# Luna attention and SMeLU feed-forward: seven add-and-max passes of batches 0 and 1 on GpSimd, and a shared clock for GpSimd's loads and passes in the planner

## The chip, the cores and the metric

One Trainium2 chip, one core. The metric is the device time of one execution in microseconds (us), the median of the runs; less is better. The engines are named PE (TensorE, matrix products), DVE (VectorE), ACT (ScalarE), POOL (GpSimd) and SP (SyncE, which only issues transfers). Each works through its own queue in order, and they wait for each other on semaphores.

## The reference

```python
# q, k, v: (8, 8, 576, 64), p: (8, 8, 32, 64), all float32
def sm_attn(qq, kk, vv):                    # softmax attention, scale 1/8
    s = scale * np.matmul(qq, kk.transpose(0, 1, 3, 2))
    a = np.exp(s - np.max(s, axis=-1, keepdims=True))
    a = a / (np.sum(a, axis=-1, keepdims=True) + 1e-09)
    return np.matmul(a, vv)
p_packed = sm_attn(p, k, v)                 # 32 landmarks look at 576 keys
x = sm_attn(q, p_packed, p_packed)          # 576 queries look at the landmarks
x = x.transpose(0, 2, 1, 3).reshape(4608, 512)
h = x @ w_in                                # 512 -> 2048
g = np.where(h >= 1, h, np.where(h <= -1, 0.0, (h + 1) ** 2 / 4))   # SMeLU
out = g @ w_out                             # 2048 -> 512, (4608, 512) float32
```

## The kernel before, in words

There are eight batches of 576 tokens. For each batch the kernel turns k and q (`kT`, `qT`), makes the scores of the landmarks (`sp`, `ex`), the packed values (`pk`, `ppT`), the scores of the queries and their softmax (`s2`, `eT`, `sm`, `ln`, `rc`, `A`). Instead of the attention's output it then forms M = packed values times w_in (`mp`, evicted to `M`), so that the hidden layer is h = A times M directly.

The hidden layer of a batch is worked in KF = 16 tiles fi of 128 hidden units by 576 tokens, each in the function `hidden`, by four steps:

- `mm` (L649, PE): four matmuls into the PSUM tile h
- `low` (L655, ACT): x = Prelu(h - 1) with slope 0.5, from PSUM to float32 in SBUF
- `cut` (L663 on DVE or L665 on ACT): t = max(x + 1, 0), float32 from SBUF to SBUF. This is the add-and-max pass.
- `last` (L670, DVE): min(t, 1) * t, written as bfloat16 into hT

The result is the SMeLU: for h above 1 it is 1 * h, between it is t * t with t = (h + 1) / 2. In batch 0 the first two tiles (`SPLIT = 2`) are worked in two halves of 288 tokens each. An output tile (function `output`, L723) takes 128 tokens of hT and sums 16 matmuls, one for each fi, into the PSUM tile o. It is evicted to ob by ACT or DVE (L197, the line of the helper `copy`) and stored by SP (L741). Batches are paired; a pair has nine output tiles of 128 tokens.

The order of all work is written by a planner (`Task`, `Plan`) before anything is emitted. Each step is a task with a rank, the tasks that it needs, the buffers that it takes, and its possible engines, each with how long the engine is kept and when the result is there. `Plan.run` simulates the engines, and always gives the engine that is free first the lowest rank that is ready. The order found is the order in which the instructions are emitted, so every engine's queue is fixed by it, and so is the engine of each step with a choice (t among them: DVE or ACT). The ranks come from constants: `H1, H2` and `PITCH0, PITCH1` for the hidden tiles, `T1, T2` and the offsets beside them for the attention of batches 1 and 2, `L1` for the landmarks of batches 2 to 7, `M1` for the pitch of M's groups in batch 0, `EARLY` for the output tiles that belong to batches 0 and 1 (start and span of each one's 16 matmuls).

Nearly all loads are issued from GpSimd's queue (`G_.dma_start`, L274 for k, q and v, L285 and L290 for the weights, L293 for p). The plan keeps their clock under the name DMA (0.78 us for an issue) and GpSimd's one other task, `make_identity`, under POOL: two clocks for one engine. Where the plan expects PE to wait before the first output matmul, `warm` puts products of zeros (L791) into PE's queue; here they are called filler.

```python
t_t = plan.add(r + 0.02, {"DVE": (0.16 + 0.3 / n, 0.156 + 0.3 / n, part(cut)),
                          "ACT": (0.12 + 0.48 / n, 0.21 + 0.48 / n, part(cut))}, [t_x], ...)
```

Here n is 2 for a tile that is worked in halves and 1 otherwise.

Of the kernel before, what the change touches and what calls it, by code (L numbers as in the profile page):

```python
# [24 lines left out]
class Plan:  # L25
# [25 lines left out]
    def run(self, slack):  # L51
        waiting = {id(t): len(t.deps) + len(t.behind) for t in self.tasks}
        for t in self.tasks:
            for d in t.deps + t.behind:
                d.users.append(t)
        ready = [t for t in self.tasks if not waiting[id(t)]]
        done = []
        while ready:
            best = None
            found = defaultdict(list)  # L60
            left = {b: sorted(v) for b, v in self.slots.items()}
            for t in sorted(ready, key=lambda t: t.rank):
                at = max((d.end + self.LATENCY for d in t.deps), default=0.0)
                at = max([at] + [d.start + 0.001 for d in t.behind])
                need = defaultdict(int)
                for b in t.takes:
                    need[b] += 1
                short = any(len(left[b]) < n for b, n in need.items())
                wants = at < self.free["PE"] + self.CLAIM
                for b, n in need.items():  # L70
                    if not short:
                        at = max(at, left[b][n - 1] + self.LATENCY)
                    if wants:
                        del left[b][:n]
                if short:
                    continue
                for e in t.ways:
                    found[e].append((max(self.free[e], at), t))
            for e, some in found.items():
                first = min(x[0] for x in some)  # L80
                at, t = min((x for x in some if x[0] <= first + slack.get(e, 0.0)), key=lambda x: (x[1].rank, x[0]))
                if best is None or at < best[0]:
                    best = at, t, e
            assert best is not None, "no step can take its buffers"
            at, t, e = best
            if e == "PE" and t.mode != self.mode:
                at = max(at, self.free[e] + self.SWITCH)
            ready.remove(t)
            keep, lasts = t.ways[e][:2]
            t.start, t.engine = at, e  # L90
            if e == "DMA":
                begin = max(self.pipe, at + lasts)
                self.pipe = begin + t.ways[e][3]
                t.end = self.pipe + t.ways[e][4]
            else:
                t.end = at + lasts
                if len(t.ways[e]) > 3:

                    beside = self.pipe > at + 1.5
                    self.pipe = max(self.pipe, at + 1.5) + t.ways[e][3] * (1.4 if beside else 1.0)  # L100
                    t.end = max(t.end, self.pipe + t.ways[e][4] * (2.0 if beside else 1.0))
            self.free[e] = at + keep
            if e == "PE":
                self.mode = t.mode
            for b in t.takes:
                self.slots[b].remove(min(self.slots[b]))
            for box in t.frees:
                box[0] -= 1
                box[1] = max(box[1], t.end)
                if box[0] == 0:  # L110
                    self.slots[box[2]].append(box[1])
            done.append(t)
            for u in t.users:
                waiting[id(u)] -= 1
                if waiting[id(u)] == 0:
                    ready.append(u)
        assert len(done) == len(self.tasks)
        return sorted(done, key=lambda t: t.start)
# [3 lines left out]
def kernel(  # L122
# [14 lines left out]
    ALU = mybir.AluOpType  # L137
# [19 lines left out]
    MB1 = {("w_in", 0, 0): 0.7, ("w_in", 0, 1): 0.7}  # L157
    FIRST = 2
    PAIRED = 2
    SPLIT, AHALF, WPARTS, MPARTS, QLATE, ORDER3, ORDER, MERGE = 2, 0, 1, 2, 0, 4, 2, 2  # L160
    Q0 = [range(0, 8, 2), range(1, 5, 2), range(5, 9, 2)]
    LOADS = "k0 v0 q0 win0 win1 win2 k1 wout0 v1 wout1 win3 wout2 q1 wout3 q2 v2 k2 p"
    H1, H2 = 22.12, 44.98
    PITCH0, PITCH1 = 2.02, 0.20
    T1, T2 = -12.12, 26.79
    LENT = [2, 5]
    L1, M1 = -0.94, -0.23
    KT1, QT1 = -5.40, 11.05
    SC1, PK1 = 23.87, 1.56
    ST1, MT1 = 34.14, 40.50  # L170
    EARLY = [[(11.06, 92.69), (49.64, 36.28), (46.46, 38.0), (38.16, 25.3)], [(56.52, 5.8), (23.31, 23.03), (58.69, 13.54), (38.34, 20.24), (1.0, 50.02)]]

    V, A_, G_ = nc.vector, nc.scalar, nc.gpsimd
    nc.scalar.preload_act_table_set("natural_log_exp_and_others")
# [14 lines left out]
    plan = Plan(dict(BUFS, dma=8))  # L189
# [167 lines left out]
    def attention(b, at, fine):  # L357
# [110 lines left out]
        def packed(e):  # L468
# [15 lines left out]
            for g in range(G):  # L484
                for c in range(NC):
# [3 lines left out]
        t = plan.add(at["pk"], {"PE": (1.01, 1.18, packed) if paired else (1.28, 1.45, packed)},  # L489
                     [ready["ex0"], ready["ex1"], consts] + (pairs if paired else landed["v", b, 0]),  # L490
                     ["w", "ppT"], mode=None if paired else "pk")
# [43 lines left out]
        for gs in [[0], [1]] if fine else [[0, 1]]:  # L535
            needs = {id(t): t for g in gs for h in range(g, H, G) for t in ready["q", h]}

            def small(e, gs=gs):
                probs(gs)
                if merged:  # L540
# [3 lines left out]
            t = plan.add(at["s2"] + 0.01 * gs[0], {"PE": (long, long + 0.15, small)},  # L544
                         (pp if len(gs) > 1 else [pp[gs[0]]]) + list(needs.values()) + [landed["w_in", 3]] * merged,
                         ["w", "eT"] * len(gs) + ["w", "M"] * merged, mode="s")
# [6 lines left out]
        for g in range(G):  # L553
# [24 lines left out]
            r = at["sm"] + 0.2 * g  # L578
# [6 lines left out]
            n = 2 if AHALF and b == 0 else 1  # L585
# [32 lines left out]
        for fs in groups:  # L618

            parts = [[0], [1]] if WPARTS and (b, fs) == (0, [0]) else [[0, 1]]  # L620
            r = at["M"] + at.get("M+", 2.0) * fs[0]
            copies = defaultdict(list)
            for i, gs in enumerate(parts):
                needs = [landed["w_in", 0, g] if WPARTS and f == 0 else landed["w_in", f] for f in fs for g in gs]
                t = plan.add(r + 0.02 * i, {"PE": (0.24 * len(fs), 0.24 * len(fs) + 0.17,
                                                   lambda e, fs=fs, gs=gs: project(fs, gs))},
                             pp + needs, ["w"] * len(fs) * (i == 0) + (["M"] if (fs[0], i) == (0, 0) else []),
                             mode="s", behind=[before])
                before = t
                mms.append(t)  # L630
                for f in fs:
                    copies[f] += taken(r + 0.02 * i, t, f, gs)
            for f in fs:
                plan.release("w", copies[f])
# [6 lines left out]
    def hidden(b, fi, rank):  # L641
# [16 lines left out]
        def cut(e, hs):  # L658
            if hs[0] == 0:
                have["t", b, fi] = new("t", [P, 2, HALF], f32)  # L660
            x, t = (have[n, b, fi][:, hs[0]:hs[-1] + 1] for n in "xt")
            if e == "DVE":
                V.tensor_scalar(t, x, 1.0, 0.0, ALU.add, ALU.max)  # L663
            else:
                nc.scalar.activation(t, x, AF.Relu, bias=1.0)  # L665

# [11 lines left out]
        for hs in parts:  # L678
            n, r = len(parts), rank + 0.005 * hs[0]

            def part(f, hs=hs):
                return lambda e: f(e, hs)

            t_h = plan.add(r, {"PE": (0.49 / n, 0.165 + 0.49 / n, part(mm))},
                           (A_of[b][hs[0]::n] if AHALF else A_of[b]) + M_of[b, fi], ["w"] if hs[0] == 0 else [])
            t_x = plan.add(r + 0.01, {"ACT": (0.14 + 0.48 / n, 0.17 + 0.48 / n, part(low))}, [t_h], ["x"] if hs[0] == 0 else [])
            t_t = plan.add(r + 0.02, {"DVE": (0.16 + 0.3 / n, 0.156 + 0.3 / n, part(cut)),
                                      "ACT": (0.12 + 0.48 / n, 0.21 + 0.48 / n, part(cut))}, [t_x], ["t"] if hs[0] == 0 else [])
            t_g = plan.add(r + 0.03, {"DVE": (0.07 + 0.6 / n, 0.157 + 0.6 / n, part(last))}, [t_t] + old)
            for nm, t in zip("hxtg", (t_h, t_x, t_t, t_g)):  # L690
                done[nm].append(t)
# [70 lines left out]
    for b in range(B):  # L762
        if b == 2:
            landmarks(2, B, L1, [landed["p"], identity])
        attention(b, stages(b), b == 0)
        pitch = lasts[b] / KF
        for fi in range(KF):
            hidden(b, fi, base[b] + pitch * fi)
        plan.release("M", h_of[b])
        plan.release("A", h_of[b])  # L770
        first = 0 if b % 2 == 0 else 4
        for j, (start, span) in enumerate(EARLY[b] if b < len(EARLY) else evenly(4 + b % 2, base[b] + SPAN, SPAN)):
            parts = 2 if (b, first + j) == (B - 1, 8) else 1
            output(b // 2, first + j, start, span / KF / parts, parts)
# [52 lines left out]
```

## Time and profile before

| what | value |
|---|---|
| median of 3 runs | 246.28 us (246.12 to 247.0) |
| profiled execution | 246.44 us, of which the span of its instructions 244.7 us |
| PE busy | 96% of the span |
| ACT busy | 80% |
| DVE busy | 72% |
| POOL busy | 12%, in 42 instructions |
| granted TensorE clock | 1.0 |

A row of a timeline gives start, duration, engine, line, operation, what is written and read, shapes, how many instructions are merged, and in brackets the idle time of the engine before them with what ended it. Rows of merged instructions overlap those of their neighbours a little, since the end of a matmul is its pipeline's end. A row of the groups gives after the bar the busy time of all, the mean of one in ns, and after the next bar the idle time before them. Matmuls count as busy while they are in the pipeline, so that PE's busy share says little about short waits; the chain of waits, which follows the work that ended last backwards, and the timeline say more.

### The profile page before, as it was taken

The numbers are of one execution on the slowest core, as the hardware profiler recorded it, in microseconds if no ns is written. First come the engines' busy times: TensorE is split into PE (matmuls) and PEld (weight loads), VectorE is DVE, ScalarE is ACT, GpSimd is POOL, SyncE is SP. The second block draws the span as 40 slices with busy tenths as digits, with TensorE's granted clock in tenths as the row PEclk, the third lists the DMA queues.
The fourth block names the chain that finished last, engine by engine and source line by source line (L and its number), as shares of the span: only waits on it lengthen the run. The fifth ranks groups of instructions, "written<-read, shape, count | busy, mean of one in ns | idle before, by whom it ended". The sixth has DMA issues, their size and how long they took to land.

```text
span 244.7 us, 5478 instructions
## 1 busy us (share of the span) xinstructions
PE 235.9 (96%) x2185; PEld 137.1 (56%) x2222; DVE 177.0 (72%) x301; ACT 196.8 (80%) x332; POOL 29.0 (12%) x42
## 2 busy tenths in 40 slices
PE   8999989999999999999999999999999999999993
PEld 2645646465545665566465546655565455555453
DVE  4548985579978996799899559948996877775000
ACT  3586988899969987998999799899978998876111
POOL 8452130000130030031003001100000000000000
PEclk9999999999999999999999999999999999999999
DMA  7999999999399999999999999967611111122223
GB/s 163 197 206 205 205 207 204 203 156 172 116 151 237 202 169 194 214 162 216 232 148 163 240 165 135 182 120 139 142 44 46 43 46 44 43 54 79 54 75 86
DMA packets 59194, 35.85 MB, mean 147 GB/s; under 512 B 31904, under 2 KB 54688, under 8 KB 59168
## 3 DMA queue, kind: packets, MB, share of 16 engines
q0 software_dynamic: 24256, 18.25, 50.6%
q1 hardware_dynamic: 34208, 16.69, 33.9%
q10 hardware_dynamic: 704, 0.56, 0.8%
q8 instruction: 17, 0.28, 0.5%
q14 instruction: 9, 0.07, 0.1%
HBM read 37.22 MB, written 9.44 MB: 191 GB/s over the span
## 4 chain that ended last, share of the span: by engine, by line
PE 85%; DVE 5%; DMA 4%; issue 3%; ACT 2%; POOL 1%; POOLq 0%
PE o L723 47%; PE h L649 24%; DMA q<-in_q_dram 4%; PE mp L529 3%; PE o L791 2%; DVE hT L670 2%; PE sp L431 2%; PE sm L561 2%; PE pk L476 1%; DVE t L663 1%; PE s L516 1%; PE tp L377 1%; DVE M L197 1%; ACT x L655 1%; PE pk L486 1%
## 5 line engine op out<-in xcount | busy, mean ns | idle before, releaser
L723 PE MATMUL o<-w_out_sb,hT 128*128 128x512 bf16 (+1 forms) x559 | 142.3, 373 | 2.1 <-issue 0.8
L670 DVE SCALAR_TENSOR_TENSOR hT<-t 128x576 bf16<-128x576 f32 (+1 forms) x130 | 94.0, 745 | 9.1 <-ACT t L665 7.0
L655 ACT ACTIVATE x<-h 128x576 f32<-128x576 f32 (+1 forms) x130 | 78.9, 654 | 7.4 <-PE h L649 5.7
L723 PEld LDWEIGHTS <-hT 128*128 128x128 bf16 x592 | 55.6, 98 | 49.0 <-issue 5.8
L649 PE MATMUL h<-A,M 128*128 128x288 bf16 x512 | 78.8, 286 | 0.3
L649 PEld LDWEIGHTS <-M 128*128 128x128 bf16 x512 | 49.5, 98 | 27.2 <-issue 0.7
L665 ACT ACTIVATE t<-x 128x576 f32<-128x576 f32 (+1 forms) x62 | 42.9, 694 | 1.0
L663 DVE TENSOR_SCALAR t<-x 128x576 f32<-128x576 f32 (+1 forms) x68 | 31.0, 456 | 10.5 <-ACT x L655 10.4
L197 ACT CAST M<-mp 128x1024 bf16<-128x1024 f32 (+1 forms) x20 | 19.1, 991 | 5.1 <-PE mp L529 5.0
L197 ACT COPY ob<-o 128x512 f32<-128x512 f32 (+1 forms) x19 | 11.0, 577 | 14.7 <-PE o L723 14.5
L197 DVE CAST M<-mp 128x1024 bf16<-128x1024 f32 (+1 forms) x14 | 15.5, 1108 | 4.1 <-PE mp L529 4.1
L575 DVE SCALAR_TENSOR_TENSOR A<-eT,rs,rc 128x576 bf16<-128x576 bf16 x16 | 12.5, 815 | 7.2 <-ACT rc L570 7.2
L197 DVE COPY ob<-o 128x512 f32<-128x512 f32 x18 | 12.4, 691 | 6.4 <-PE o L723 5.8
L274 POOL DMA_DIRECT2D k<-in_k_dram x8 | 6.2, 779 | 75.6 <-DMA kT<-k 51.9
L791 PE MATMUL o<-zeros 128*128 128x512 bf16 (+1 forms) x42 | 13.3, 435 | 1.4 <-DVE zeros L227 1.2
L437 ACT ACTIVATE ex<-sp 96x768 bf16<-96x768 f32 x16 | 12.2, 801 | 1.9 <-PE sp L431 1.9
L556 ACT ACTIVATE eT<-s,rs 128x576 bf16<-128x576 f32 x16 | 11.0, 740 | 1.5 <-PE s L516 1.3
L274 POOL DMA_DIRECT2D v<-in_v_dram x8 | 6.8, 849 | 43.1 <-DVE vv L463 37.0
L529 PE MATMUL mp<-w_in_sb,ppT 64*32 64x512 bf16 x256 | 10.7, 380 | 0.8 <-DVE M L197 0.8
L197 ACT CAST ppT<-pk 64x128 bf16<-64x128 f32 x22 | 5.7, 260 | 6.8 <-PE pk L486 6.5
L565 ACT ACTIVATE ln<-sm 128x576 f32<-128x576 f32 x16 | 10.2, 652 | 0.5
L570 ACT ACTIVATE rc<-ln 128x576 f32<-128x576 f32 x16 | 10.3, 682 | 0.1
(50 smaller groups left out, 115.4 us busy)
## 6 DMA issues: line engine op xcount, KB each, us to landing
v<-in_v_dram POOLq DMA_DIRECT2D x8, 576.0 KB, 11.4
out_dram<-ob SPq DMA_DIRECT2D x23, 192.0 KB, 3.1
k<-in_k_dram POOLq DMA_DIRECT2D x7, 576.0 KB, 7.8
q<-in_q_dram POOLq DMA_DIRECT2D x7, 576.0 KB, 14.6
out_dram<-ob SPq DMA_DIRECT2D x24, 128.0 KB, 2.4
w_out_sb<-in_moe_w_out_dram POOLq DMA_DIRECT2D x4, 512.0 KB, 19.8
w_in_sb<-in_moe_w_in_dram POOLq DMA_DIRECT2D x3, 512.0 KB, 13.9
out_dram<-ob SPq DMA_DIRECT2D x23, 64.0 KB, 2.2
```

Of the source, the lines that this page charges most:

```text
L197: i = (nc.vector.tensor_copy if e == "DVE" else nc.scalar.copy)(to, of)
L274: G_.dma_start(tokens(nm, b)[:, heads(hs)], rows_of(nm, b, hs))
L437: nc.scalar.activation(have["ex", b][:, :, 64 * i:64 * i + 64], have["sp", b, i][:TP, :E * X * G], AF.Exp, scale=scale)
L529: nc.tensor.matmul(have["mp", b, f][a * NP:(a + 1) * NP, g], have["ppT", b][r, g, a], w_in_sb[r, a, f * FW:(f + 1) * FW], start=True, stop ...
L575: V.scalar_tensor_tensor(have["A", b][:, g, xs], have["eT", b, g][:, xs], rs_of[b][:, g, :1], have["rc", b, g][:, xs], ALU.mult, ALU.mult)
L649: nc.tensor.matmul(have["h", b, fi][:, hf, :HALF], have["M", b][:, g, fi * P:(fi + 1) * P], have["A", b][:, g, hf], start=(g == 0), stop=( ...
L655: nc.scalar.activation(have["x", b, fi][:, hs[0]:hs[-1] + 1], have["h", b, fi][:, hs[0]:hs[-1] + 1, :HALF], AF.Prelu, bias=-1.0, alpha=0.5)
L663: V.tensor_scalar(t, x, 1.0, 0.0, ALU.add, ALU.max)
L665: nc.scalar.activation(t, x, AF.Relu, bias=1.0)
L670: V.scalar_tensor_tensor(dst, t, 1.0, t, ALU.min, ALU.mult)
L723: nc.tensor.matmul(have["o", key][:, :w], hT[:, fi, i * P:(i + 1) * P], w_out_sb[:, fi, cols], start=(fi == 0), stop=(fi == KF - 1))
L791: nc.tensor.matmul(o[:, :w], zeros[:, :P], zeros[:, :w], start=True, stop=True)
```

## The change

Seven passes t of the hidden layer are given to GpSimd: tiles fi with fi % 4 = 1 in batches 0 and 1, save the ones that are worked in halves (tile 1 of batch 0). For these tiles the plan has no choice of engine, and books 1.1 us of GpSimd for one. The plan now sets the clocks of loads (DMA) and of GpSimd's other work (POOL) together, after each task of either. Apart from that only ranks are changed: the constants T2, L1, M1 and EARLY, and a new list JOG that moves the rank of single hidden tiles of batch 0 and of single groups of M in batches 0 and 1.

```diff
             self.free[e] = at + keep
+            if e in ("DMA", "POOL"):
+                self.free["DMA"] = self.free["POOL"] = at + keep
...
-    SPLIT, AHALF, WPARTS, MPARTS, QLATE, ORDER3, ORDER, MERGE = 2, 0, 1, 2, 0, 4, 2, 2
+    SPLIT, AHALF, WPARTS, MPARTS, QLATE, ORDER3, ORDER, MERGE, POOLED = 2, 0, 1, 2, 0, 4, 2, 2, 4
...
-    T1, T2 = -12.12, 26.79
+    T1, T2 = -12.12, 30.63
...
-    L1, M1 = -0.94, -0.23
+    L1, M1 = -1.91, 2.02
...
-    EARLY = [[(11.06, 92.69), (49.64, 36.28), (46.46, 38.0), (38.16, 25.3)], [(56.52, 5.8), (23.31, 23.03), (58.69, 13.54), (38.34, 20.24), (1.0, 50.02)]]
+    JOG = [[0.0, -1.0, 0.0, 0.0, -2.9, 0.0, ...], [0.0, ...], [0.0, 1.2, 0.0, 0.0, 0.0, 0.2, 0.0, -1.1]]
+    EARLY = [[(13.98, 89.75), (49.64, 36.28), (48.61, 35.68), (38.16, 25.3)], [(56.52, 5.8), (22.14, 12.87), (62.17, 11.69), (38.34, 20.24), (1.0, 50.02)]]
...
-            r = at["M"] + at.get("M+", 2.0) * fs[0]
+            r = at["M"] + at.get("M+", 2.0) * fs[0] + (JOG[2][4 * b + fs[0]] if b < 2 else 0.0)
...
-            if e == "DVE":
-                V.tensor_scalar(t, x, 1.0, 0.0, ALU.add, ALU.max)
+            if e != "ACT":
+                (V if e == "DVE" else G_).tensor_scalar(t, x, 1.0, 0.0, ALU.add, ALU.max)
...
-            t_t = plan.add(r + 0.02, {"DVE": (0.16 + 0.3 / n, 0.156 + 0.3 / n, part(cut)),
-                                      "ACT": (0.12 + 0.48 / n, 0.21 + 0.48 / n, part(cut))}, [t_x], ["t"] if hs[0] == 0 else [])
+            ways = {"DVE": (0.16 + 0.3 / n, 0.156 + 0.3 / n, part(cut)), "ACT": (0.12 + 0.48 / n, 0.21 + 0.48 / n, part(cut))}
+            if b < 2 and n == 1 and fi % POOLED == 1:
+                ways = {"POOL": (1.1, 1.15, part(cut))}
+            t_t = plan.add(r + 0.02, ways, [t_x], ["t"] if hs[0] == 0 else [])
...
-            hidden(b, fi, base[b] + pitch * fi)
+            hidden(b, fi, base[b] + pitch * fi + (JOG[b][fi] if b < 2 else 0.0))
```

More of the change, by code (lines that the diff above doesn't have):

```diff
@@ L170 @@
     ST1, MT1 = 34.14, 40.50
-    EARLY = [[(11.06, 92.69), (49.64, 36.28), (46.46, 38.0), (38.16, 25.3)], [(56.52, 5.8), (23.31, 23.03), (58.69, 13.54), (38.34, 20.24), (1.0, 50.02)]]
+    JOG = [[0.0, -1.0, 0.0, 0.0, -2.9, 0.0, 0.0, 0.0, 0.0, 0.0, 0.0, 0.0, 0.0, 0.0, 0.0, 0.0], [0.0, 0.0, 0.0, 0.0, 0.0, 0.0, 0.0, 0.0, 0.0, 0.0, 0.0, 0.0, 0.0, 0.0, 0.0, 0.0], [0.0, 1.2, 0.0, 0.0, 0.0, 0.2, 0.0, -1.1]]
+    EARLY = [[(13.98, 89.75), (49.64, 36.28), (48.61, 35.68), (38.16, 25.3)], [(56.52, 5.8), (22.14, 12.87), (62.17, 11.69), (38.34, 20.24), (1.0, 50.02)]]
     V, A_, G_ = nc.vector, nc.scalar, nc.gpsimd
```

## The prediction, made before the changed kernel was run

> **What bounds the kernel now.** I read the page first: the busy shares, the slices, the groups. Then a table of windows, then the timelines of TensorE, VectorE and GpSimd between 20 and 92 us, the waits of TensorE, and the chain of waits.
>
> ```profile
> span 244.7 us, 5478 instructions
> PE 235.9 (96%) x2185; PEld 137.1 (56%) x2222; DVE 177.0 (72%) x301; ACT 196.8 (80%) x332; POOL 29.0 (12%) x42
> ...
> L670 DVE SCALAR_TENSOR_TENSOR hT<-t 128x576 bf16<-128x576 f32 (+1 forms) x130 | 94.0, 745 | 9.1 <-ACT t L665 7.0
> ...
> L665 ACT ACTIVATE t<-x 128x576 f32<-128x576 f32 (+1 forms) x62 | 42.9, 694 | 1.0
> L663 DVE TENSOR_SCALAR t<-x 128x576 f32<-128x576 f32 (+1 forms) x68 | 31.0, 456 | 10.5 <-ACT x L655 10.4
> ```
>
> TensorE is the bound over the whole span: 235.9 of 244.7 us. GpSimd does almost nothing but issue loads. The pass that moves is t (add 1, cut at 0): today 68 times on VectorE at 456 ns and 62 times on ScalarE at 694 ns. But a kernel that TensorE bounds gains only where TensorE waits or does filler, so I looked for such places.
>
> ```profile
> 20.25 2.14 PE L649 MATMUL h<-A,M 128*128 128x288 bf16 x16
> 22.22 0.27 PE L791 MATMUL o<-zeros 128*128 128x256 bf16 x1
> 22.77 0.72 PE L791 MATMUL o<-zeros 128*128 128x512 bf16 x3
> 23.32 1.64 PE L649 MATMUL h<-A,M 128*128 128x288 bf16 x12
> 25.00 0.60 PE L791 MATMUL o<-zeros 128*128 128x512 bf16 x2
> 29.62 0.65 PE L649 MATMUL h<-A,M 128*128 128x288 bf16 x4
> 36.37 0.41 PE L529 MATMUL mp<-w_in_sb,ppT 64*32 64x512 bf16 x8 [0.59 <-DVE M L197]
> ...
> PE o L791 <- DVE zeros L227: 1.2, 1, 1.2
> PE mp L529 <- DVE M L197: 0.8, 2, 0.6
> PE tp L377 <- DMA q<-in_q_dram: 0.2, 1, 0.2
> PE o L723 <- issue: 0.2, 1, 0.2
> ```
>
> L791 is filler: products of zeros, put where the plan expects TensorE to wait. After the first h tiles (four matmuls of a row x16 each, from 20.25 us; tiles 4 to 6 are the x12 at 23.32, tile 9 the x4 at 29.62) there are three stretches of it. Their rows overlap their neighbours a little; in the chain of waits they take 0.11, 0.65 and 0.60 us:
>
> ```profile
> 22.39 0.11 PE o L791
> 22.83 0.65 PE o L791 x3
> 25.00 0.60 PE o L791 x2
> ```
>
> That is 1.36 us. With the 0.59 us wait of mp at 36.37, where TensorE waited for a VectorE eviction, it makes 1.95 us: all that I find to win in the stretch where t moves, since the last four lines, the waits of TensorE from 0 to 92 us, hold besides only the start of the filler at the head, another 0.2 us of mp and two pieces of 0.2 us.
>
> The other question is how much room the engines have that the change leans on.
>
> ```profile
> 25.00:30.00 5.00, 4.94 (x67) 3.62 (x68) 5.00 (x10) 5.00 (x10) 0.79 (x1) 1.00 1.28 204
> 30.00:35.00 5.00, 4.95 (x96) 2.92 (x95) 4.20 (x8) 4.71 (x11) 2.43 (x3) 1.00 1.24 207
> ...
> 50.00:55.00 5.00, 4.95 (x34) 3.30 (x34) 4.40 (x8) 4.70 (x9) 0.00 (x0) 1.00 1.10 133
> 55.00:60.00 5.00, 4.95 (x49) 2.85 (x49) 4.82 (x10) 4.83 (x9) 0.00 (x0) 1.00 1.20 151
> 60.00:65.00 5.00, 4.93 (x33) 2.82 (x32) 4.90 (x9) 4.84 (x9) 0.00 (x0) 1.00 0.75 205
> ```
>
> Columns: stretch, length, then busy time of PE, weight load, VectorE, ScalarE and GpSimd, the granted clock (1.00), DMA. Most of batch 0's tiles stand in the first two rows, most of batch 1's in the last three. VectorE and ScalarE are full together with TensorE. Over 50 to 65 us VectorE is idle for 15 - (4.40 + 4.82 + 4.90) = 0.88 us. And the chain shows that TensorE waits on VectorE's last pass there with nothing to spare:
>
> ```profile
> 61.05 0.77 DVE hT L670
> 61.82 0.05 issue
> 61.87 0.60 PE o L723 x2
> ```
>
> So a VectorE delay in batch 1 becomes a TensorE delay, and TensorE, full to the end of the span, doesn't give it back.
>
> **The change, part by part.** Which tiles: every tile with fi = 1, 5, 9, 13, in batches 0 and 1, unless it is split in two; batch 0's tile 1 is split (SPLIT = 2). So seven passes move: 5, 9, 13 of batch 0, and four of batch 1.
>
> *What GpSimd needs for one.* The trace has no such pass on GpSimd. Its nearest rows are the constants of the start:
>
> ```profile
> 0.24 0.10 POOL L811 MEMSET const-float32-0.0<- 128x1 f32 x1 [0.24 <-issue]
> ...
> 3.17 0.29 POOL masks.py:199 TENSOR_SCALAR_AFFINE_SELECT ident<-ident 128x128 bf16<-128x128 bf16 x1
> ```
>
> One element takes 0.10 us, 128 elements with a read and a write 0.29 us: (0.29 - 0.10) / 128 = 1.5 ns an element, so 576 elements take 0.10 + 576 x 1.5 ns = 0.96 us. Ends: 1.30 us if the whole 0.29 us scales (0.29 x 4.5), and 0.46 us if GpSimd were as fast as VectorE. I take 0.96 us, as the row that reads and writes is the closest in kind; the planner's 1.10 us in the diff lies between. The Trainium skill, "GPSIMD Engine Reference", section 3.1, has a best case of 512 elements in 769 ns, which for 576 would be an estimate of 0.87 us; no run here shows it yet, and the sum would hardly differ.
>
> *What it takes off.* The plan chooses the engine of t freely, so about two of batch 1's four passes leave VectorE: 2 x 0.46 = 0.9 us; the two others leave ScalarE (2 x 0.69 = 1.4 us). Of batch 0's first two, one each: 0.46 us off VectorE.
>
> *What it adds on VectorE.* This is the disputed cost. GpSimd works beside t or hT of VectorE in a few places of the trace, while it issues loads:
>
> ```profile
> 33.19 0.91 POOL L293 DMA_DIRECT2D p_nat<-in_p_dram  x1
> 66.23 0.77 POOL L274 DMA_DIRECT2D v<-in_v_dram  x1 [32.14 <-DVE vv L463]
> 90.21 0.90 POOL L274 DMA_DIRECT2D v<-in_v_dram  x1
> ...
> 33.64 0.74 DVE L663 TENSOR_SCALAR t<-x 128x576 f32<-128x576 f32 x1
> 66.53 0.73 DVE L663 TENSOR_SCALAR t<-x 128x576 f32<-128x576 f32 x1
> 90.28 0.45 DVE L663 TENSOR_SCALAR t<-x 128x576 f32<-128x576 f32 x1
> 65.86 0.75 DVE L670 SCALAR_TENSOR_TENSOR hT<-t 128x576 bf16<-128x576 f32 x1
> ```
>
> The t at 33.64 took 0.74 us and that at 66.53 0.73 us, against a mean of 456 ns: 0.28 us longer, both begun inside a GpSimd row. If they were held at their start and then ran 0.456 us, they were let go at 33.92 and 66.80 us, 0.73 and 0.57 us after GpSimd began: 80% and 74% of its row. The t at 90.28 was not held; there the GpSimd row is 0.90 us, 0.13 us longer than its neighbours of 0.77. So the two engines exclude each other for most of a GpSimd row, and the later one pays. The hT at 65.86, running as GpSimd began, took its usual 0.75 us.
>
> The lower end of the cost is thus nothing (GpSimd always comes second), the upper the whole pass, 0.96 us, or 1.30 us at its slow price. I take 78% of 0.96 = 0.75 us a tile, by the two rows in which t was held. That hT would be held as t was is not shown by any row here; I assume it, as hT reads two operands from the same memory.
>
> The Trainium skill, "SBUF — State Buffer", section "Who interferes with whom", speaks against this change: VectorE's two-port modes exclude any GpSimd instruction, and VectorE instructions with two SBUF inputs exclude a GpSimd instruction that reads SBUF, the later one blocking until the other has finished. The two held rows agree with the first half; no row here shows the second. By that rule the cost per tile would be the whole pass, which is the second rival below.
>
> *Sum for batch 1.* VectorE gains 4 x 0.75 = 3.0 us and loses 0.9: +2.1 us, into 0.88 us of room: 1.2 us reach TensorE. What is queued behind a held VectorE instruction is the next t and hT and, mixed among them, evictions; TensorE waits for these in the fixed order of its queue.
>
> *Sum for batch 0.* Tiles 5 and 9, by their matmuls, fall at about 25 to 31 us: 2 x 0.75 - 0.46 = 1.0 us more on VectorE, which is busy 5.00 of 5 us up to 30 and has 0.80 us idle from 30 to 35. About half of that room comes after the work that waits, so 0.6 us reach TensorE. Tile 13 falls where VectorE has long been idle and costs nothing while this cover stands (0.75 - 0.46 = 0.3 us without it):
>
> ```profile
> 39.39 0.46 DVE L663 TENSOR_SCALAR t<-x 128x576 f32<-128x576 f32 x1 [2.41 <-ACT x L655]
> ```
>
> *Loads behind a pass.* GpSimd's queue is in order: a pass that waits for its x holds the next load's issue. Those from 25.08 (batch 2's q) to 33.19 us (p) stand between tiles 5, 9 and 13. I cost it at nothing: loads queue for long, 14.6 us in the median from issue to landing for q, so an issue 1 us late lands where it would have. Without that cover it is 1 us per late issue, for batch 2's attention.
>
> ```profile
> 25.08 0.79 POOL L274 DMA_DIRECT2D q<-in_q_dram  x1 [2.64 <-PE h L649]
> ...
> q<-in_q_dram POOLq DMA_DIRECT2D x7, 576.0 KB, 14.6
> ```
>
> *The shifted ranks (T2, L1, M1, JOG, EARLY) and the shared clock for loads and passes in the plan* change only the order of the same work and the number of fillers. Between 0 and the 1.95 us found above they can win; the first moved pass (tile 5) comes after the filler at 25.00, so moving it frees nothing ahead of it, and only another order can. I take 0.4 us, a fifth. To the other side, an order built on a VectorE that is never held can lose what stands above, so no separate term.
>
> Net: 1.2 + 0.6 - 0.4 = +1.4 us. The profiled execution took 246.44 us, its span 244.7 and 1.7 us around it; the sum makes that 247.8. The median of the runs, 246.28, lies 0.16 us lower, so I predict 247.7 us, +0.6%. Bounds of this case: a hold of 0.6 us a tile takes off 6 x 0.15 = 0.9 us, a hold of 0.9 us adds as much: 246.8 to 248.6.
>
> **The rivals.** *Faster: the relief reaches TensorE.* If a hold costs VectorE under 0.45 us a tile in batch 1 ((0.9 + 0.88) / 4, the point where it decides), nothing is lost there, ScalarE has 1.4 us less to do, and the plan can draw h tiles forward into the filler at 22 to 26 us. Winning all 1.36 us of it gives 244.9; the further 0.59 at 36.37 is unlikely, as an M eviction on VectorE ends it. For: ScalarE and VectorE full at 25 to 30; the unheld t at 90.28. Against: tile 5 is later than the filler; two of three overlaps held. Chance 0.22.
>
> *A full hold.* VectorE pays the whole pass: 4 x 0.96 - 0.9 - 0.88 = 2.1 us in batch 1, 2 x 0.96 - 0.46 - 0.4 = 1.1 us in batch 0, less 0.4: +2.8, 249.1 us; at 1.30 us a pass, 2.0 us more: 251.1. This is what the skill's rule above gives. For: both engines wait for each other in turn, since hT of the tile needs the pass. Against: 74% and 80% in the two rows. Chance 0.12.
>
> *Nothing to see.* Holds fall on VectorE's waits and on evictions from PSUM, and the new order pays for the rest: 246.3 us. For: the plan books GpSimd 1.10 us, so hT isn't queued at once behind it. Against: the full windows. It also covers the case that the change doesn't do what it says, the seven passes being only reshuffled. Chance 0.24.
>
> **How the numbers follow.** The forecast has 0.42. About 0.5% (1.23 us) is what a measurement of this kernel can tell from no change, so the bounds are 245.05 and 247.51. Forecast: 0.34 slower, 0.08 same. Full hold: 0.12 slower. Nothing to see: 0.24 same. Faster rival: 0.17 faster, 0.05 same, when only part of the filler goes. Together 0.17 faster, 0.37 same, 0.46 slower. The range reaches from the faster rival's 244.9 to 250.0, beyond the full hold's 249.1 but short of its end with the slow price; cases of both signs hold most of the chance, so the forecast's own range is 246.8 to 248.6.
>
> **What would show it.** Seven TENSOR_SCALAR rows on POOL of about 0.96 us. VectorE rows of t or hT that begin inside them should be longer by up to 0.75 us, so hT's mean between 50 and 65 us above 745 ns, and idle time of TensorE before o or h released by hT. Wrong, if those hT rows keep 0.75 us, if GpSimd's rows stretch instead, or if filler after 20 us falls from 1.36 us towards none while TensorE has no new waits; if batch 2's loads land late, the cover of the loads was gone.

## The result and the profile after

The changed kernel takes 250.25 us in the median of four runs (249.65 to 250.59), the kernel before 246.33: a ratio of 1.0154, interval 1.0134 to 1.0174. It is slower by 3.8 us, where +1.4 was forecast. The span of the profiled execution grew from 244.7 to 248.4 us.

The head of the page after, and its groups for hT and t (after the bar: busy time, mean ns, then idle time before them):

```profile
span 248.4 us, 5531 instructions
PE 239.2 (96%) x2222; PEld 136.9 (55%) x2222; DVE 179.6 (72%) x300; ACT 194.5 (78%) x326; POOL 45.2 (18%) x49
...
L674 DVE SCALAR_TENSOR_TENSOR hT<-t 128x576 bf16<-128x576 f32 (+1 forms) x130 | 94.3, 747 | 12.4 <-ACT t L669 7.6
...
L669 ACT ACTIVATE t<-x 128x576 f32<-128x576 f32 (+1 forms) x59 | 40.8, 694 | 1.0
L667 DVE TENSOR_SCALAR t<-x 128x576 f32<-128x576 f32 (+1 forms) x64 | 30.9, 482 | 10.1 <-ACT x L659 9.9
...
L667 POOL TENSOR_SCALAR t<-x 128x576 f32<-128x576 f32 x7 | 16.4, 2341 | 23.5 <-ACT x L659 20.9
```

The seven passes are there, and each takes 2.34 us: not my 0.96, and not the 1.10 that the plan books. Over the whole run VectorE has four passes t fewer (68 to 64) and ScalarE three (62 to 59). The next fence has VectorE's waits for GpSimd between 20 and 75 us (total, number, longest), and the chain of waits around batch 0's tile 13.

```profile
DVE hT L674 <- POOL t L667: 2.6, 4, 1.2
...
39.21 0.66 ACT x L659
39.87 0.08 issue
39.95 2.65 POOL t L667
42.59 0.02 issue
42.62 0.77 DVE hT L674
```

VectorE reaches the hT of a moved tile and stands idle until GpSimd is through: 2.6 us in four waits. The chain now leads through GpSimd. I had counted tile 13 as covered by idle time.

Where TensorE pays is seen in its weight loads (PEld), one for each matmul. Their waits for VectorE between 20 and 92 us, first before, then after:

```profile
PEld L723 <- DVE hT L670: 1.6, 5, 0.5
PEld L516 <- DVE qT L197: 0.4, 1, 0.4
PEld L431 <- DVE kT L197: 0.3, 1, 0.3
```

```profile
PEld L729 <- DVE hT L674: 3.4, 7, 1.0
PEld L520 <- DVE qT L201: 1.5, 2, 1.2
PEld L435 <- DVE kT L201: 0.8, 1, 0.8
```

That is 1.8 us more for hT, 1.1 for qT and 0.5 for kT, all behind VectorE. The lines show what TensorE waits for, and the sum of 3.4 us is no account of the span's 3.7: the waits of the matmuls themselves grew only from 0.8 to 2.6 us, and the short pass that is booked rightly, below, has 3.1 us of such waits for hT and loses 0.7 us. qT and kT are evictions of the next batch's attention that stand in VectorE's queue behind a late hT or a held t. The windows after, for the last two stretches of the prediction's table, show TensorE and ScalarE idle together where both had been full:

```profile
55.00:60.00 5.00, 4.17 (x43) 2.13 (x42) 4.92 (x8) 3.23 (x6) 2.78 (x2) 1.00 0.92 136
60.00:65.00 5.00, 4.73 (x31) 2.75 (x30) 4.62 (x8) 4.31 (x7) 0.85 (x1) 1.00 1.29 126
```

The filler didn't go. Both pages count 2222 weight loads, one for each matmul, so there is as much of it as before (the page before lacks some matmul records), and its rows after 20 us stand in the same places:

```profile
22.14 0.27 PE L797 MATMUL o<-zeros 128*128 128x256 bf16 x1
22.68 0.71 PE L797 MATMUL o<-zeros 128*128 128x512 bf16 x3
24.71 0.81 PE L797 MATMUL o<-zeros 128*128 128x512 bf16 x3
```

### The profile page after: what moved, and what is told of

Its sections match the earlier page's. It is cut to its first block, busy times and chain, and to the rows that moved or that the text cites. A ratio compares the mean times of both kernels' runs of the same rounds, so it can differ in the third digit from the quotient of the medians.

```text
span 248.4 us, 5531 instructions
## 1 busy us (share of the span) xinstructions
PE 239.2 (96%) x2222; PEld 136.9 (55%) x2222; DVE 179.6 (72%) x300; ACT 194.5 (78%) x326; POOL 45.2 (18%) x49
## 4 chain that ended last, share of the span: by engine, by line
PE 79%; DVE 8%; issue 4%; POOL 3%; DMA 3%; ACT 2%; POOLq 0%
PE o L729 45%; PE h L653 20%; DVE hT L674 4%; PE mp L533 3%; POOL t L667 3%; DMA k<-in_k_dram 3%; PE sp L435 2%; PE o L797 2%; PE pk L480 2%; DVE t L667 2%; PE sm L565 1%; ACT x L659 1%; PE s L520 1%; PE pk L490 1%; PE tp L381 1%
## 5 line engine op out<-in xcount | busy, mean ns | idle before, releaser
L729 PE MATMUL o<-w_out_sb,hT 128*128 128x512 bf16 (+1 forms) x592 | 148.4, 374 | 1.4 <-DVE hT L674 0.9
L669 ACT ACTIVATE t<-x 128x576 f32<-128x576 f32 (+1 forms) x59 | 40.8, 694 | 1.0
L201 ACT CAST M<-mp 128x1024 bf16<-128x1024 f32 (+1 forms) x19 | 18.0, 991 | 4.1 <-PE mp L533 4.0
L667 POOL TENSOR_SCALAR t<-x 128x576 f32<-128x576 f32 x7 | 16.4, 2341 | 23.5 <-ACT x L659 20.9
L201 DVE CAST M<-mp 128x1024 bf16<-128x1024 f32 (+1 forms) x15 | 16.7, 1114 | 3.8 <-PE mp L533 3.8
L201 ACT CAST ppT<-pk 64x128 bf16<-64x128 f32 x20 | 5.2, 260 | 6.3 <-PE pk L490 5.9
```

The source lines that it names most:

```text
L201: i = (nc.vector.tensor_copy if e == "DVE" else nc.scalar.copy)(to, of)
L667: (V if e == "DVE" else G_).tensor_scalar(t, x, 1.0, 0.0, ALU.add, ALU.max)
L729: nc.tensor.matmul(have["o", key][:, :w], hT[:, fi, i * P:(i + 1) * P], w_out_sb[:, fi, cols], start=(fi == 0), stop=(fi == KF - 1))
```

## Experiments

Theory A: the pass is longer than booked, and hT waits for it. Theory B: GpSimd holds VectorE. Theory C: the new ranks cost. Ratios are to the kernel before, with their intervals.

### The ranks, the passes, and a shorter pass

**Order only**: all new ranks, no pass on GpSimd.

```diff
-            if b < 2 and n == 1 and fi % POOLED == 1:
+            if False:
```

> The changed kernel with all its new ranks, but no pass on GpSimd: every t has the choice of VectorE or ScalarE again. Theories A and B (the passes cost the time): 245.8 to 247.3 us, as the kernel before within 0.4%. Theory C (the new ranks themselves cost, whatever GpSimd does): 248.5 us or more.

Measured: 246.15 us, 0.9994 (0.9978 to 1.0011). Theory C falls. A win by the ranks isn't seen either, though the interval admits one of 0.5 us.

**Passes only**: the ranks of before, the rest as changed.

```diff
-    T1, T2 = -12.12, 30.63
+    T1, T2 = -12.12, 26.79
...
+    JOG = [[0.0] * 16, [0.0] * 16, [0.0] * 8]
```

> The seven passes on GpSimd and the shared clock in the plan, with the ranks of the kernel before (T2, L1, M1, EARLY as before, JOG all zero). Theories A and B: 249 to 251.5 us, the loss is there without the new ranks. Theory C: 246 to 247.5 us.

Measured: 251.0 us, 1.0203 (1.0157 to 1.0249). The loss is in the passes; it is 0.8 us larger than with the new ranks, but the intervals overlap.

**Half a pass**: GpSimd does 288 of the 576 tokens, ScalarE the rest.

```diff
+                if e == "POOL":
+                    G_.tensor_scalar(t[:, :1], x[:, :1], 1.0, 0.0, ALU.add, ALU.max)
+                    nc.scalar.activation(t[:, 1:], x[:, 1:], AF.Relu, bias=1.0)
...
```

> The changed kernel with the plan untouched; of each of the seven passes GpSimd does the first 288 tokens and ScalarE the other 288 (0.47 us more for ScalarE at the same place of its queue). So GpSimd's part comes near the 1.10 us that the plan books. Theory A (the length beyond the booked one is what costs): 246.3 to 247.8 us, GpSimd's rows 1.1 to 1.3 us, and the waits of VectorE's hT for GpSimd gone. Theory B (VectorE's holds cost, and stretch the passes): half of the holds stay, 248 to 249 us.

Measured: 247.23 us, 1.0039 (1.0027 to 1.0051); the groups of 20 to 75 us:

```profile
L678 DVE SCALAR_TENSOR_TENSOR hT<-t 128x576 bf16<-128x576 f32 x30 | 22.0, 762 | 1.0 <-POOL t L668 0.6
L668 POOL TENSOR_SCALAR t<-x 128x288 f32<-128x288 f32 x7 | 9.6, 1377 | 27.4 <-ACT x L659 25.2 <-DVE t L671 2.2
```

At 1.38 us a pass the wait of hT fell from 2.6 to 0.6 us and three quarters of the loss went. Half a pass halves the holds too, as shown below, so this run alone doesn't part A from B.

### How long a pass is, and why

**A probe**: extra passes ahead of the loads, and eight after the last load beside a working VectorE.

```diff
+    pr = const.tile([P, 2, HALF], f32)
...
+    for i in range(3):
+        G_.tensor_scalar(pr, pr, 1.0, 0.0, ALU.add, ALU.max)
+    for i in range(2):
+        G_.tensor_scalar(pr[:, :1], pr[:, :1], 1.0, 0.0, ALU.add, ALU.max)
...
```

> The kernel before, with thirteen extra GpSimd passes whose result is not used: at the very start, ahead of the loads, three of 128x576 and two of 128x288, in place on a scratch tile, with VectorE idle or setting constants; and eight of 128x576 after the last load, beside VectorE's t and hT of the late batches. It is made for the length of the passes, not for its time (the loads start late). Theory A (a pass takes over 2 us by itself): the three at the start follow each other at 2.0 to 2.4 us, the halves at 1.0 to 1.3, the late eight at 2.2 to 2.7. Theory B (a pass takes about 1 us by itself and is stretched by VectorE's use of the shared memory path): 0.9 to 1.2 us at the start, 2.2 to 2.7 late. In both, rows of VectorE's t beside the late passes show holds, by up to 0.5 us over 0.456; whether hT (0.745) is held is open.

Rows of GpSimd:

```profile
1.40 6.88 POOL L193 TENSOR_SCALAR pr<-pr 128x576 f32<-128x576 f32 x3
8.36 2.43 POOL L195 TENSOR_SCALAR pr<-pr 128x288 f32<-128x288 f32 x2
...
165.73 19.12 POOL L805 TENSOR_SCALAR pr<-pr 128x576 f32<-128x576 f32 x8
```

By itself a pass takes 6.88 / 3 = 2.29 us, a half 2.43 / 2 = 1.22; beside VectorE 19.12 / 8 = 2.39. So the length is GpSimd's own, as theory A has it, and VectorE stretches it by a twentieth in the mean. The slope is (2.29 - 1.22) / 288 = 3.7 ns an element; I had taken 1.5.

**Other operations**: the same probe with two passes each of max alone, copy, add-max, add-multiply; in a second kernel of add-min, multiply-greater, add-max on bfloat16, subtract-max.

```diff
...
+    for i in range(2):
+        G_.tensor_scalar_max(pr, pr, 0.0)
+    for i in range(2):
+        G_.tensor_copy(pr, pr)
...
+    for i in range(2):
+        G_.tensor_scalar(pr, pr, 1.0, 0.5, ALU.add, ALU.mult)
```

> The kernel before with eight extra GpSimd passes of 128x576 float32, in place on a scratch tile, ahead of the loads, two of each kind: max alone, a copy, add and max, add and multiply. Made for their lengths, not for its time. If the length comes from two operations in one pass: max alone and the copy take about half of 2.29 us, 1.0 to 1.3, and add-multiply as long as add-max. If it is the reading and writing of 576 float32 elements: all four take 2.1 to 2.4 us. If it is max: add-multiply is clearly shorter than add-max.

> Lengths again, two extra passes of each kind ahead of the loads of the kernel before: add and min, multiply and is-greater, subtract and max, all 128x576 float32, and add and max on 128x288 bfloat16. If max has a slow way of its own: add-min is slow too or not, subtract-max 2.1 to 2.3 us. If every comparison is slow: multiply-greater and add-min about 2 us as well. If max is slow by float32 alone: the bfloat16 pass takes about 0.4 us, else 1.1 to 1.3.

GpSimd's rows of the first, in the order named, and the groups of the second (add-min, multiply-greater, subtract-max, bfloat16):

```profile
1.41 3.91 POOL L193 TENSOR_SCALAR pr<-pr 128x576 f32<-128x576 f32 x2
5.38 1.39 POOL L195 COPY pr<-pr 128x576 f32<-128x576 f32 x2
6.85 4.36 POOL L197 TENSOR_SCALAR pr<-pr 128x576 f32<-128x576 f32 x2
11.29 1.42 POOL L199 TENSOR_SCALAR pr<-pr 128x576 f32<-128x576 f32 x2
```

```profile
L195 POOL TENSOR_SCALAR pr<-pr 128x576 f32<-128x576 f32 x2 | 4.6, 2301 | 0.2
L197 POOL TENSOR_SCALAR pr<-pr 128x576 f32<-128x576 f32 x2 | 4.3, 2152 | 0.2
L201 POOL TENSOR_SCALAR pr<-pr 128x576 f32<-128x576 f32 x2 | 4.3, 2134 | 0.1
L199 POOL TENSOR_SCALAR pb<-pb 128x288 bf16<-128x288 bf16 x2 | 2.4, 1176 | 0.1
```

Copy and add-multiply take 0.7 us, everything with max, min or a comparison 1.9 to 2.3 us. The shape is not it, nor the count of operations: max alone costs 1.96, add and multiply together 0.71. A bfloat16 half takes as long as a float32 half.

### What GpSimd does to VectorE

**Shadow passes**: the kernel before; GpSimd runs the pass again for the same seven tiles, into a scratch tile.

```diff
...
+            if b < 2 and len(hs) == 2 and fi % 4 == 1:
+                G_.tensor_scalar(pr, x, 1.0, 0.0, ALU.add, ALU.max)
```

> The kernel before, every t where it was on VectorE or ScalarE; for the same seven tiles GpSimd runs the pass a second time, from the same x into a scratch tile that nobody reads. Nobody waits for GpSimd, save x's buffer (four of them) and the loads behind it in GpSimd's queue; VectorE has the holds. Theory A (the wait for a pass of 2.3 us costs): 246.2 to 247.3 us, since the eight late passes of the first experiment held VectorE by 2.3 us in all, 0.28 us each, so 4 x 0.28 = 1.1 us in batch 1 against 0.88 us of idle time. Theory B (holds cost most of the loss): 248.5 us or more.

Measured: 248.95 us, 1.0106 (1.0081 to 1.0130). So GpSimd's passes cost 2.6 us where nobody waits for them and nothing is taken off VectorE, and theory A alone falls. Two passes, and VectorE's rows inside them:

```profile
52.40 2.21 POOL L668 TENSOR_SCALAR pr<-x 128x576 f32<-128x576 f32 x1 [8.89 <-ACT x L656]
...
66.79 2.30 POOL L668 TENSOR_SCALAR pr<-x 128x576 f32<-128x576 f32 x1 [2.33 <-ACT x L656]
```

```profile
52.54 0.92 DVE L664 TENSOR_SCALAR t<-x 128x576 f32<-128x576 f32 x1
53.49 1.43 DVE L673 SCALAR_TENSOR_TENSOR hT<-t 128x576 bf16<-128x576 f32 x2
...
67.01 1.10 DVE L673 SCALAR_TENSOR_TENSOR hT<-t 128x576 bf16<-128x576 f32 x1
68.03 0.55 DVE L464 COPY vv<-v 96x1536 bf16<-96x1536 bf16 x1
68.50 0.74 DVE L673 SCALAR_TENSOR_TENSOR hT<-t 128x576 bf16<-128x576 f32 x1
```

In each of the seven passes one t or hT is held, by 0.46 us (four t, 0.92) or 0.35 us (three hT, 1.10); what follows, still inside the pass, runs at its usual length. It is the first that starts inside, save in the pass at 56.34 us: there an hT at 56.47 took its usual 0.75 us, the t behind it was held, and GpSimd's own row is the longest of the seven, 2.87 us. One hold for a pass, not 78% of it.

**Shadow of half the size**, and **shadow with add-multiply** (0.7 us in place of 2.3):

```diff
-                G_.tensor_scalar(pr, x, 1.0, 0.0, ALU.add, ALU.max)
+                G_.tensor_scalar(pr[:, :1], x[:, :1], 1.0, 0.0, ALU.add, ALU.max)
```

```diff
-                G_.tensor_scalar(pr, x, 1.0, 0.0, ALU.add, ALU.max)
+                G_.tensor_scalar(pr, x, 1.0, 1.0, ALU.add, ALU.mult)
```

> As the fifth experiment (the kernel before, with seven passes of GpSimd that nobody waits for), but each over 288 of the 576 tokens, so about 1.22 us by itself. That run lost 2.7 us, with about 0.43 us of hold for each pass, on one VectorE instruction each. If there is one hold for a pass whatever its length: 248.2 to 249.3 us, and 0.35 to 0.47 us of hold for each pass. If the hold goes with the length of the pass: 247.2 to 248.0 us, about 0.2 us each.

> As the fifth experiment (the kernel before, and seven GpSimd passes that nobody waits for), with add-multiply, about 0.7 us, in place of add-max. If the hold goes with the length: 0.12 us a pass, 246.2 to 247.2 us, in line with 248.95 at 2.3 us and 247.36 at 1.2 us. If a hold falls on what starts early in a pass, by a fixed amount: 247.4 us or more.

Measured: 247.36 us, 1.0044 (1.0030 to 1.0058), and 248.18 us, 1.0083 (1.0067 to 1.0099). VectorE's t between 20 and 75 us in the full, the half and the add-multiply shadow:

```profile
L664 DVE TENSOR_SCALAR t<-x 128x576 f32<-128x576 f32 x17 | 9.9, 581 | 4.1 <-ACT x L656 4.1
```

```profile
L664 DVE TENSOR_SCALAR t<-x 128x576 f32<-128x576 f32 x17 | 9.3, 544 | 4.1 <-ACT x L656 4.1
```

```profile
L664 DVE TENSOR_SCALAR t<-x 128x576 f32<-128x576 f32 x17 | 9.9, 581 | 4.1 <-ACT x L656 4.1
```

The hold is the same, 581 ns in the mean, for passes of 2.3 and of 0.7 us, and smaller for half the elements. It goes with the data that a pass moves, not with its time. My rule for the third shadow, a hold by the length, fell. As its holds are those of the full shadow, the price of holds alone is the 2.0 us that it lost; whether the full shadow's 0.6 us more come from the length (the loads behind a pass, the buffers of x) these runs don't tell, since the two intervals overlap.

### Length and holds in the changed kernel's own queues

**On VectorE**: the plan and every queue's order as changed, the seven passes emitted on VectorE. **Without max**: the same queues, GpSimd adds 1 and multiplies by 1 (the cut at 0 of seven tiles is left out).

```diff
-                (V if e == "DVE" else G_).tensor_scalar(t, x, 1.0, 0.0, ALU.add, ALU.max)
+                V.tensor_scalar(t, x, 1.0, 0.0, ALU.add, ALU.max)
```

```diff
+                if e == "POOL":
+                    G_.tensor_scalar(t, x, 1.0, 1.0, ALU.add, ALU.mult)
...
```

> The changed kernel with the same order of every step (the plan still books GpSimd 1.10 us), but the seven passes are emitted on VectorE, at the place in its queue where the plan starts them on GpSimd. VectorE has 7 x 0.456 = 3.2 us more to do, ScalarE nothing more, there are no holds and no waits of 2.3 us. Theory A: most of the 4 us goes, 246.3 to 248.0 us, as VectorE's extra 0.456 us a pass is a fifth of 2.3. A theory by which the queues that the plan wrote for an unloaded VectorE cost the time (C'): 249 us or more.

> The changed kernel, in which the seven GpSimd passes add 1 and multiply by 1 in place of add and max: the cut at 0 is left out in these tiles. Such a pass took 0.7 us in the ninth experiment, where add-max took 2.2. All queues are the same. If the max on GpSimd, and so the length beyond the 1.10 us booked, is the cause: 245.5 to 247.0 us, no wait of hT for GpSimd, and holds of VectorE of at most 0.2 us a pass. If holds and queues matter whatever the length: 248 us or more.

Measured: 246.58 us, 1.0011 (0.9996 to 1.0026), and 247.38 us, 1.0050 (1.0034 to 1.0067). With the first, the theory that the queues alone cost (C') falls. The groups of the second, 20 to 75 us:

```profile
L677 DVE SCALAR_TENSOR_TENSOR hT<-t 128x576 bf16<-128x576 f32 x30 | 22.3, 773 | 0.3
L670 DVE TENSOR_SCALAR t<-x 128x576 f32<-128x576 f32 x12 | 6.6, 552 | 3.8 <-ACT x L659 3.8
L668 POOL TENSOR_SCALAR t<-x 128x576 f32<-128x576 f32 x7 | 6.2, 892 | 29.4 <-ACT x L659 29.3
```

At 0.89 us a pass, below the booked 1.10, no hT waits for GpSimd. In one and the same order the loss is thus 0.3 us with the passes on VectorE (the interval includes none), 1.2 us with a short pass on GpSimd, 3.8 us with the real one: a short pass costs 0.9 us more on GpSimd than on VectorE, and 2.6 us go with the length. The wait of hT was as long (2.6 us). The short pass lies between the two cases that I had set: the wait is gone, the holds are larger than 0.2 us a pass (0.34 us for an hT at 31.72 us, 0.46 us for a t at 55.44).

When the loss arises shows in a step that both orders hold, the sums sm of the softmax of batches 1 and 2; with the passes on VectorE, then in the changed kernel:

```profile
44.58 0.41 PE L565 MATMUL sm<-eT,onesblk 128*128 128x288 bf16 x2
...
72.84 0.41 PE L565 MATMUL sm<-eT,onesblk 128*128 128x288 bf16 x2
```

```profile
46.06 0.41 PE L565 MATMUL sm<-eT,onesblk 128*128 128x288 bf16 x2
...
76.40 0.41 PE L565 MATMUL sm<-eT,onesblk 128*128 128x288 bf16 x2
```

The changed kernel is 1.5 us late at batch 1's sums and 3.6 us late at batch 2's, and its span ends 3.6 us later: the loss is made among the hidden tiles of batches 0 and 1, and nothing of it is given back.

**The true cost in the plan**, with the new ranks and with the old:

```diff
-                ways = {"POOL": (1.1, 1.15, part(cut))}
+                ways = {"POOL": (2.35, 2.4, part(cut))}
```

> The changed kernel with all its ranks, and the plan books for a GpSimd pass what was measured, 2.35 us (result at 2.40) in place of 1.10 (1.15). Theory A as a fault of the booking alone: 246.0 to 247.3 us, the steps are ordered around the long pass. If the length itself is the matter and no order of these ranks hides it (A with no cover): 248 to 250 us.

> As the run before, with the ranks of the kernel before. Theory A as a fault of the booking alone: 246.3 to 247.8 us, well under the 251.0 us that these ranks gave with 1.10 us booked. With no cover: 249 us or more.

Measured: 246.76 us, 1.0019 (1.0007 to 1.0030), and 246.54 us, 1.0008 (0.9999 to 1.0018). Booked rightly, the long pass costs almost nothing: VectorE's wait for GpSimd is down to this in the first of the two, and gone in the second.

```profile
DVE hT L674 <- POOL t L667: 0.2, 1, 0.2
```

But neither wins anything. That the holds and the relief about cancel is my reading; no run has the relief without the holds.

**Short pass, rightly booked** (add-multiply; the cut left out):

```diff
-                ways = {"POOL": (1.1, 1.15, part(cut))}
+                ways = {"POOL": (0.72, 0.78, part(cut))}
```

> As the thirteenth, and the plan books 0.72 us (result at 0.78) for such a pass. It shows what the change could win if GpSimd had a pass of the length of a plain one: by the prediction's room for winning, 1.95 us at the most, 244.9 to 246.3 us; if nothing is to be won since TensorE is full anyway, 246.0 to 246.6.

Measured: 246.87 us, 1.0031 (1.0020 to 1.0042). Outside both cases, on the slow side. Even a GpSimd pass of 0.83 us (the mean of its rows here) wins nothing; why it loses 0.7 us was not traced.

### Where

**One batch alone** (`b < 1`, and in the other kernel `b == 1`):

```diff
-            if b < 2 and n == 1 and fi % POOLED == 1:
+            if b < 1 and n == 1 and fi % POOLED == 1:
```

> The changed kernel with GpSimd's pass in batch 0 alone (three tiles, 1.10 us booked). By the count of tiles, 3/7 of the 3.9 us: 247.9 us. By the prediction's places (batch 0 has idle time behind tile 13): a third, 247.5 us.

> The changed kernel with GpSimd's pass in batch 1 alone (four tiles, 1.10 us booked). By the count, 4/7 of 3.9 us: 248.5 us. By the prediction's places, two thirds: 248.8 us.

Measured: 248.05 us, 1.0078 (1.0059 to 1.0096), and 249.04 us, 1.0118 (1.0088 to 1.0148). Batch 0 has 2.0 of the two losses' 4.9 us, 40%, between the third by the prediction's places and the 43% by the count, which these runs can't tell apart. The two add up to 4.9 us against 3.8 for the whole; the plan orders each kernel anew, and the intervals allow for most of the difference.

No version beat the kernel before; order only and it are the same.

## Why the prediction was wrong

The sign and the place were right: VectorE's delay in batches 0 and 1 became TensorE's and wasn't given back. The size was not: +1.4 us against +3.8, and 250.25 lies just above the range's 250.0. What failed is the length of the pass, and with it a wait that the sum put at nothing. The run without max shows this: with a pass of 0.89 us, near the 0.96 that I had assumed, the same queues lose 1.2 us, near my +1.4. That this comes so close is in part luck, since its terms were off both ways. By its steps:

- *What GpSimd needs for one* failed. 0.96 us was scaled from a row of 128 elements of another operation; 2.34 us were measured, above my upper end of 1.30. The operation decides: a copy or an add-multiply of this shape takes 0.7 us. The booked 1.10 looked like a confirmation, and was as wrong.
- *hT waiting for the pass* had no term. I let it be covered since the plan books 1.10 us, so the term hung on the first one. It is the largest: 2.6 us of VectorE's time, and 2.6 us of the loss go with the length.
- *What it adds on VectorE* was too dear: 0.75 us a tile, against 0.46 us for a held t and 0.35 us for a held hT, one a pass in the shadows, and 0.1 to 0.47 us in the changed kernel. That hT is held too, which I had assumed, the shadows showed. The Trainium skill's "SBUF — State Buffer", section "Who interferes with whom", agrees in that both kinds of VectorE instruction are held; that the later one blocks until the other has finished does not fit rows of 0.92 us inside a pass of 2.21 us, and the measurement decides.
- *What it takes off* was too small: t on VectorE between 20 and 75 us fell from 17 to 12, 5 x 0.456 = 2.3 us against my 0.9 + 0.46 = 1.4.
- *The shifted ranks* were credited 0.4 us; order only shows none (0.9994), but its interval (0.9978 to 1.0011) doesn't exclude it.
- *Tile 13 costs nothing* failed: VectorE waited 1.19 us there, the longest wait of the four, and qT stood behind it.
- *Loads behind a pass* held: v's issue slid from 31.66 to 34.01 us, and the one wait of TensorE on a load after 20 us (0.4 us, for batch 1's k) is for a load issued at 11 us, ahead of every pass.
- *Faster* as a rival fell with the last two bookings: neither the true cost nor a short pass brought the filler's 1.36 us. Both kernels still hold the same seven products of filler after 20 us, so no order here drew work into it. That TensorE, nearly full from 25 us on, has little use for the relief is my reading.

With the measured terms, VectorE between 20 and 75 us has 2.6 us of waiting for GpSimd. Holds lengthen its t by 12 x (622 - 456) = 2.0 us, hT by 30 x (764 - 754) = 0.3 and the copy vv by 3 x (697 - 548) = 0.45, against 0.5 us of holds on t before (a few of the held t, as that at 26.17 us, begin beside a load's issue and not a pass); relief takes off 2.3. That is 2.5 us; the rest of the 3.7 us of span, 1.2 us, I have no closed account for: hT, kT and qT come late in an order that was made for earlier ones, and what each lateness costs TensorE wasn't measured one by one. The means are these, after and before:

```profile
L674 DVE SCALAR_TENSOR_TENSOR hT<-t 128x576 bf16<-128x576 f32 x30 | 22.2, 764 | 3.0 <-POOL t L667 2.6
L667 DVE TENSOR_SCALAR t<-x 128x576 f32<-128x576 f32 x12 | 7.5, 622 | 3.6 <-ACT x L659 3.6
L467 DVE COPY vv<-v 96x1536 bf16<-96x1536 bf16 x3 | 2.0, 697 | 0.0
```

```profile
L670 DVE SCALAR_TENSOR_TENSOR hT<-t 128x576 bf16<-128x576 f32 x30 | 22.1, 754 | 0.5
L663 DVE TENSOR_SCALAR t<-x 128x576 f32<-128x576 f32 x17 | 8.3, 488 | 4.1 <-ACT x L655 4.1
L463 DVE COPY vv<-v 96x1536 bf16<-96x1536 bf16 x4 | 2.1, 548 | 0.0
```

## What to carry to other kernels

Measure an operation on its engine, alone and at its shape, before a planner books it: here one row at the start of the kernel would have shown 2.29 us for 1.10, and with the true number the same change cost 0.1 to 0.2% in place of 1.5%. In a fixed order a step that is longer than booked makes its first consumer wait; here the loss that went with the length was as large as that wait, 2.6 us, and idle time around tile 13 didn't cover it. And the relief of two full engines won nothing here, where a third one, full as well, sets the end.

## What the runs showed of the hardware

- On GpSimd a pass over 128x576 float32 took 0.7 us as a copy or as add-multiply, and 1.9 to 2.3 us with max, min or a comparison; in bfloat16 288 elements took 1.18 us, as in float32 (1.17 to 1.22).
- A GpSimd pass of the long shadow held one VectorE instruction, by 0.46 us (t) or 0.35 us (hT) at 576 elements. The holds were as large where the pass took 0.7 us, and 0.22 to 0.29 us (t) at 288 elements. It is no rule without exception: in the probe the first of the late passes has two held rows, an hT of 1.10 and a t of 1.25 us. A VectorE copy between tiles (vv) can be the one held, too: 1.02 us in place of 0.55 in the changed kernel.
- VectorE hardly slowed GpSimd's long pass in the mean: 2.29 us alone, 2.39 us beside it. Single passes differ more: 2.13 to 2.87 us in the long shadow, and 0.67 to 1.42 us in the one with add-multiply, so GpSimd pays at times as well.
